# A table of shifted priorities in a kernel whose instruction order is made by a list scheduler

## The chip, the cores and the metric

The kernel runs on one core of a Trainium2 chip. The metric is the device time of one execution in microseconds; three runs of the kernel before gave 1033.35 as their median. Engines are named as in the profile: PE (TensorE), DVE (VectorE), ACT (ScalarE), POOL (GpSimd) and SP (SyncE, which here only issues DMAs).

## What is computed

Hash-masked attention for 4 batches of 8 heads (768 positions, 64 dimensions), and a gated two-layer product on its output. The weights come in as 64-bit floats.

```python
q_bits = (np.einsum('bhsd,dk->bhsk', q, proj) > 0)     # 6 bits, k likewise
mask = q_bucket[:, :, :, None] == k_bucket[:, :, None, :]
scores = np.where(mask, scale * q @ k.T, -1e9)
attn = exp(scores - max); attn /= attn.sum(-1) + 1e-9
x = (attn @ v).transpose(0, 2, 1, 3).reshape(B * S, H * D)   # 3072 x 512
out = (sigmoid(x @ w_gate) * (x @ w_val)) @ w_out            # inner width 1536
```

## The kernel before

**Two stages.** In the first, the heads are taken in 16 pairs, each pair in two groups of 384 query positions. A pair (`pair`) is loaded, q and k are transposed on PE (`turn`, L957), split into two parts of lower precision, and hashed (`hash_`, L980); DVE turns the hashes into bits (`bits_k` L998, `bits_q` L991). A group (`group`) has three blocks of queries times two heads: six scores tasks (L1043 and L1048, 8 matmuls each, into PSUM tile `sc`), for each a maximum on DVE (L1057, which also moves the scores into `e`) and an exponent on ACT (L1065); then the reciprocal of the sums (`inverse`, three small DVE instructions, L1072 to L1075), six tasks of 12 transposes (`turned`, L1098, tile `tp`), each copied by ACT or DVE (L1105, tile `ef`), and three values tasks of 8 matmuls (`values`, L1115, tile `pv`). The sum is copied (L1122, `xs`), scaled on POOL (L1125) and stored to `xd` in DRAM (L1128).

In the same stage the weights are turned from 64-bit floats into pairs of 32-bit ones (`floats`, `load_w`, `load_pair`; DVE, ACT and POOL), and the first two of the twelve 128-wide slices of the inner width are already multiplied for every (batch, group) whose attention is stored (`moe_early`, `product` L548 with tiles `zg` and `zv`, `out_product` L581 with tile `zo`). A product task is 3 matmuls, four of them a product; an output task is 3 matmuls, two for each of three row blocks.

The second stage (`products`) does the other ten slices for all batches by a Strassen-like scheme of seven products (L789, tiles `zA`, `zB`, `zD`) and output pieces (L581, tile `y`). Its weights stream in through POOL's DMA queue (L1213). Between the stages stands `switch`, which waits for the last attention store, closes the first stage's memory pools and opens the second's.

**What sets the order.** No instruction is issued where it is written. Every step is put into a `Plan` with `add`: a key, an engine (or a choice of two), a cost in ns, what it comes after, and which buffers it takes and gives. `order` then plays the whole program through in a model of the chip: whenever an engine is free, it takes the ready task with the lowest `(key, number)` whose buffers are free. PE's choice also counts a price for a change of kind (`LEAVE`, `BEGIN`) and stays in its tiling for a while (`PATIENCE`): scores and transposes use half the rows of the array, values half the columns, all else the whole array. The order in which tasks start in the model is the order in which the program is emitted; on the chip each engine then works through its queue in that order, waiting where data are not there.

Keys are formulas: about one unit for each of the 96 query blocks of the whole kernel (`t0 = i * NC + g * GT`), with offsets: scores `n`, maxima `n - 3`, exponents `n + 1.25`, transposes `t0 + LAG + 0.4 c`, the first values task of a group `t0 + LAG + 4`, and its other two `OPEN`, which is -1: a task that goes on with an open accumulation goes ahead of everything. Early products begin with 10000 and the number of their unit (8 units) and go on with `OPEN`; a second-stage chain has 20000 and its batch; the 60 warm-up matmuls at the start have 100000.

**Buffers.** Scores, transposes and hashes share three PSUM tiles of two banks (`two`). Values, early products and outputs share two single banks (`one`), of which an early product may have one (`moe`). A group's accumulation holds its bank from its first values task until the copy at L1122.

Of the kernel before, what the change touches and what calls it, by code (L numbers as in the profile page):

```python
# [40 lines left out]
RATE, LANDING = 240.0, 2000  # L41


class Task:


# [20 lines left out]
class Plan:  # L67
# [9 lines left out]

    def add(self, key, engine, ns=None, emit=None, after=(), take=(), give=(), tail=0, kind="all", behind=()):
        options = engine if isinstance(engine, list) else [(engine, ns, emit)]
        t = Task((key, len(self.tasks)), options, after, take, give, tail, kind, behind)  # L80
        self.tasks.append(t)
        return t

# [104 lines left out]
def lsh_attention_glu_kernel(ctx, tc, q, k, v, proj, w_gate, w_val, w_out, out):  # L188
# [107 lines left out]
    def busy():  # L296
# [6 lines left out]
        t=0, zt=0, ws0=0, ws1=0, ws2=0, xb=0, r0=0, r1=0, r2=0, x1=0, x4=0, x5=0, x6=0, wk2=0,  # L303
# [4 lines left out]
    add = plan.add  # L308
# [8 lines left out]
    def dma(key, nbytes, emit, engine="sp", slack=0, **kw):  # L317
        t = add(key, engine, 600, emit, tail=LANDING + int(nbytes / RATE), **kw)
        t.size, t.slack = nbytes, slack
        return t  # L320
# [7 lines left out]
    def floats(key, load, after, last, name):  # L328
# [38 lines left out]

        a = dma(key, 524288, load_, slack=3000 if last else 0, after=after, take=[place])
        b1 = add(key, "dve", 440, exponent, after=[a], take=["mid" + own])
        b2 = add(key, "act", 700, shifted, after=[b1])  # L370
        c1 = add(key, "dve", 440, mantissa, after=[b1])
        c2 = add(key, "dve", 700, whole, after=[c1])
# [214 lines left out]
    def moe_early(key, b, g, stored, pace):  # L587
# [50 lines left out]
        for j in range(J1):  # L638
            g_free[j] = prev

    def products(key, pair, prev, ends):


# [273 lines left out]
    def either(copied, n=1):  # L917
        return [
            ("act", 60 + 315 * n, lambda: copied(nc.scalar.copy)),
            ("dve", 70 + 400 * n, lambda: copied(nc.vector.tensor_copy)),  # L920
        ]

    def pair(i):
# [4 lines left out]
        two = slice(2 * hp, 2 * hp + 2)  # L928
# [36 lines left out]
        def high(n, copy):  # L965
            z[n + "h"], z[n + "l"] = (at.tile([P, S], F32R, name=f"{n}{x}{u}", tag=f"{n}{x}") for x in "hl")
            copy(ordered(z[n + "h"]), turned_(n))
# [16 lines left out]
        def hash_(n):  # L984
            z["hs", n] = ps2.tile([P, 2, 512], F32, name=f"h{n}{u}", tag="two")
            for j in range(2):
                hashed(z["hs", n], f"k{j}" if n == "k" else n, n, j)
# [7 lines left out]
        def bits_k(h):  # L995
            if h == 0:
                z["kb"] = at.tile([P, 2, GN], BF16, name=f"kb{u}", tag="kb")
            nc.vector.tensor_scalar(z["kb"][:, h], z["hs", "k"][:, h, :GN], thr_k[h], None, op0=ALU.is_gt)  # L998
# [5 lines left out]
        needs, last_turn = [], None  # L1004
        for m, n in enumerate("kq"):
            n_ = t0 - 6 + m
            last_turn = add(
                n_, "pe", NC * TH, lambda n=n: turn(n), after=[here[n], last_turn],
                take=["two"] + ["h"] * (m == 0), give=[n + "r"], kind="turn",
            )  # L1010
            a = add(n_, either(lambda copy, n=n: high(n, copy), 2), after=[last_turn])
# [3 lines left out]
        for m, n in enumerate("kq"):  # L1015
            n_ = t0 - 2.8 + m * 0.6
            a = add(n_, "pe", 6 * MM, lambda n=n: hash_(n), after=[needs[m]], take=["two"])
            if n == "k":
                needs += [
                    add(n_, "dve", 590, lambda h=h: bits_k(h), after=[a], give=["two"] * h) for h in range(2)  # L1020
                ]
            else:
                needs.append(add(n_, "dve", 990, bits_q, after=[a], give=["two"]))
        needs += swaps
# [2 lines left out]
        for g in range(NG):  # L1027
            group(i, g, z, needs, v_here)

    def group(i, g, z, needs, v_here):  # L1030
# [3 lines left out]
        gz = {}  # L1034

        def scores(t, h):

            c = slice((g * GT + t) * P, (g * GT + t + 1) * P)
            gz["sc", t, h] = sc = ps2.tile([P, 2, 512], F32, name=f"sc{u}_{t}_{h}", tag="two")
            for m, (a, x) in enumerate((("l", "h"), ("h", "l"), ("h", "h"))):  # L1040
                for j, rows in enumerate(halves):
                    q_ = z[("q" if j == h else "qs") + a]
                    nc.tensor.matmul(  # L1043
                        sc[:, j, :GN], q_[rows, c], z["k" + x][rows, h * GN : (h + 1) * GN],
                        start=(m == 0), stop=False, tile_position=(j * D, 0),
                    )
            for j, rows in enumerate(halves):
                nc.tensor.matmul(  # L1048
                    sc[:, j, :GN], z["qb"][rows, c], z["kb"][rows, h], start=False, stop=True, tile_position=(j * D, 0),
                )  # L1050

        def maximum(t, h):

            if h == 0:
                gz["st", t] = at.tile([P, 2], F32, name=f"st{u}_{t}", tag="st", bufs=stock["st"])
            gz["e", t, h] = e = at.tile([P, S], F32, name=f"e{u}_{t}_{h}", tag="e", bufs=stock["e"])
            nc.vector.tensor_scalar(  # L1057
                sp(e), gz["sc", t, h][:, :, :GN], -MASKED * SCALE, None, op0=ALU.min, op1=ALU.min,
                accum_out=gz["st", t][:, h : h + 1],
            )  # L1060

        def exponent(t, h):
            gz["su"] = sums[(i * NG + g) % len(sums)]
            e, st = gz["e", t, h], gz["st", t]
            nc.scalar.activation(  # L1065
                e, e, AF.Exp, bias=st[:, h : h + 1], scale=-1.0,
                accum_out=gz["su"][:, h * GT + t : h * GT + t + 1],
            )
# [61 lines left out]
        exps = []  # L1130
        for t in range(GT):
            n = t0 + t
            least = []
            for h in range(2):
                a = score_tasks[n] = add(
                    n + h * 0.5, "pe", 6 * MM // 2 + 165, lambda t=t, h=h: scores(t, h), after=needs + score_tasks.get("last", []),
                    take=["two", "e"] + ["st"] * (h == 0), kind="scores",
                    give=["h"] if g == NG - 1 and t == GT - 1 and h == 1 else [],
                )
                score_tasks["last"] = [a]  # L1140
                least.append(add(n - 3, "dve", 880, lambda t=t, h=h: maximum(t, h), after=[a], give=["two"]))
            for h in range(2):
                exps.append(add(
                    n + 1.25, "act", 1025, lambda t=t, h=h: exponent(t, h), after=[least[h]] + exps[:1],
                    take=["su"] if t == 0 and h == 0 else [], give=["st"] * (h == 1),
                ))
        n = t0 - 0.78
        a = add(n, "dve", 560, inverse, after=exps, take=["sv"], give=["su"])
        a = add(n, "sp", 600, told, after=[a], tail=2500, give=["sv"])
        spread_ = add(n, "sp", 1200, spread, after=[a], tail=3500, take=["rb"])  # L1150
        chunks, last = {}, None
        for c in range(NC):
            n = t0 + LAG + c * 0.4
            last = add(n, "pe", 2 * GT * TH, lambda c=c: turned(c), after=exps + [last], take=["two", "ef"],
                       give=["e"] * GT * 2 if c == NC - 1 else [], kind="turn")
            chunks[c] = add(n, either(lambda copy, c=c: whole(c, copy), 2), after=[last], give=["two"])
        n = t0 + LAG + 4
        prev = None
        for cs in [range(c, c + VB) for c in range(0, NC, VB)]:
# [3 lines left out]
                after=[prev, v_here] + [chunks[c] for c in cs], take=["one"] if first else [], kind="values",  # L1163
                give=["ef"] * VB + (["vr"] if final and g == NG - 1 else []),
            )
        a = add(n - 6, either(summed), after=[prev], take=["xs"], give=["one"])
        a = add(n - 4, "pool", 1230, divided, after=[a, spread_], give=["rb"])
# [7 lines left out]
    for i in range(len(heads)):  # L1175
        pair(i)
# [5 lines left out]
    for m, w in enumerate(order):  # L1182
        key = W_KEY + W_STEP * m + W_MORE * max(0, m - 3 * J1)
# [18 lines left out]
    def switch():  # L1202
# [5 lines left out]
                          give=["moe"] * 3 + [r for r, n in late_stock.items() for _ in range(n)])  # L1208
# [51 lines left out]
```

## Time and profile before

| | |
|---|---|
| median of three runs | 1033.35 us (1033.17 to 1033.66) |
| the profiled execution | 1032.77 us, of which the span of its instructions 1031.0 |
| granted TensorE clock | 0.999 |
| HBM | 177 GB/s over the span |
| largest groups | exponents L1065 178.7 us of ACT, maxima L1057 176.4 us of DVE, `y` L581 150.9 us of PE, `pv` L1115 140.6 us of PE |

A timeline row gives start, length, engine, line, operation, `out<-in`, and how many like it were merged; brackets hold the idle time before it and whose end ended that. Matmuls are pipelined, so lengths overlap, and the distance between two starts is what a task takes. A row of stretches gives, for a window, its length and then busy time and instructions of PE, PEld, DVE, ACT and POOL, the granted clock, the DMA share and GB/s. A row of groups gives `xcount`, then busy time and mean ns of one, then the idle time before them with its causes.

### The profile page before, as it was taken

The numbers are of one execution on the slowest core, as the hardware profiler recorded it, in microseconds if no ns is written. First come the engines' busy times: TensorE is split into PE (matmuls) and PEld (weight loads), VectorE is DVE, ScalarE is ACT, GpSimd is POOL, SyncE is SP. The second block draws the span as 40 slices with busy tenths as digits, with TensorE's granted clock in tenths as the row PEclk, the third lists the DMA queues.
The fourth block names the chain that finished last, engine by engine and source line by source line (L and its number), as shares of the span: only waits on it lengthen the run. The fifth ranks groups of instructions, "written<-read, shape, count | busy, mean of one in ns | idle before, by whom it ended". The sixth has DMA issues, their size and how long they took to land.

```text
span 1031.0 us, 20353 instructions
## 1 busy us (share of the span) xinstructions
PE 1008.5 (98%) x8172; PEld 803.3 (78%) x8172; DVE 665.1 (65%) x1257; ACT 563.4 (55%) x1024; POOL 235.9 (23%) x248
## 2 busy tenths in 40 slices
PE   9999999999999999999998999999999999999998
PEld 5666567676676676766677899999999999999997
DVE  6889898788888878777636646564326433553234
ACT  2777778787676766877745434443325232433231
POOL 2213456444544333552022000000000000000000
PEclk9999999999999999999999999999999999999999
DMA  8344466765766646544147977576445754366411
GB/s 214 88 127 132 139 186 195 249 181 172 237 198 193 195 166 201 188 159 162 38 143 308 385 285 285 207 255 222 183 167 194 253 216 164 143 242 244 168 72 62
DMA packets 114558, 196.36 MB, mean 190 GB/s; under 512 B 61216, under 2 KB 83744, under 8 KB 109344
## 3 DMA queue, kind: packets, MB, share of 16 engines
q1 hardware_dynamic: 108544, 121.66, 37.0%
q0 software_dynamic: 5760, 73.40, 19.3%
q8 instruction: 64, 1.05, 0.4%
q14 instruction: 30, 0.25, 0.1%
q10 hardware_dynamic: 160, 0.00, 0.0%
HBM read 140.51 MB, written 41.94 MB: 177 GB/s over the span
## 4 chain that ended last, share of the span: by engine, by line
PE 85%; DVE 8%; issue 3%; ACT 2%; DMA 1%; POOL 0%; SPq 0%; DVEq 0%; ACTq 0%; POOLq 0%
PE y L581 16%; PE pv L1115 11%; PE sc L1043 9%; PE zBg L789 8%; PE zBv L789 8%; PE tp L1098 5%; PE zDg L789 4%; PE zDv L789 4%; DVE e L1057 3%; PE zo L581 3%; PE zg L548 3%; PE sc L1048 3%; PE zv L548 2%; PE zAg L789 2%; PE zAv L789 2%
## 5 line engine op out<-in xcount | busy, mean ns | idle before, releaser
L1065 ACT ACTIVATE e<-e,st 128x768 f32<-128x768 f32 x192 | 178.7, 932 | 36.5 <-DVE e L1057 35.9
L1057 DVE TENSOR_SCALAR_CACHE_REDUCE e<-sc 128x768 f32<-128x768 f32 x192 | 176.4, 953 | 22.8 <-PE sc L1048 22.6
L581 PE MATMUL y<-wo,gh 128*128 128x512 f32 x480 | 150.9, 396 | 0.0
L1115 PE MATMUL pv<-ef,vr 128*64 128x384 f32 x768 | 140.6, 496 | 0.0
L1105 ACT COPY ef<-tp 128x768 f32<-128x768 f32 x117 | 92.1, 798 | 50.8 <-PE tp L1098 49.7
L1098 PEld LDWEIGHTS tp<-ident,e 64*128 64x128 f32 x2304 | 83.9, 139 | 31.5 <-issue 20.3
L581 PEld LDWEIGHTS y<-wo,gh 128*128 128x128 f32 x480 | 90.0, 187 | 15.4
L1098 PE MATMUL tp<-ident,e 64*128 64x64 f32 x2304 | 95.4, 226 | 2.4 <-DVE ef L1105 1.1
L789 PE MATMUL zBv<-x,wsv 128*128 128x384 f32 x480 | 96.5, 335 | 0.9 <-ACT t167v L797 0.9
L789 PE MATMUL zBg<-x,wsg 128*128 128x384 f32 x480 | 96.4, 335 | 0.6 <-ACT t167g L797 0.6
L581 PE MATMUL y<-wo,gl 128*128 128x512 f32 x240 | 93.2, 389 | 0.0
L1043 PE MATMUL sc<-kh,ql 64*128 64x384 f32 x192 | 85.9, 447 | 6.5 <-ACT ef L1105 2.4
L789 PEld LDWEIGHTS zBv<-x,wsv 128*128 128x128 f32 x480 | 85.4, 188 | 6.4 <-ACT t167v L797 1.3
L789 PEld LDWEIGHTS zBg<-x,wsg 128*128 128x128 f32 x480 | 85.4, 188 | 5.9 <-ACT t167g L797 0.9
L1115 PEld LDWEIGHTS pv<-ef,vr 128*64 128x64 f32 x768 | 48.4, 136 | 53.3 <-issue 47.5
L1105 DVE COPY ef<-tp 128x768 f32<-128x768 f32 x75 | 71.2, 953 | 27.2 <-PE tp L1098 26.5
L1043 PE MATMUL sc<-kh,qsl 64*128 64x384 f32 x192 | 85.9, 447 | 1.1 <-DVE ef L1105 1.0
L882 ACT CAST gh<-zt 128x384 fp32r<-128x384 f32 x80 | 40.7, 513 | 83.5 <-DVE zt L877 72.0
L1048 PE MATMUL sc<-kb,qb 64*128 64x384 bf16 x384 | 64.6, 333 | 0.0
L1043 PE MATMUL sc<-kl,qh 64*128 64x384 f32 x192 | 64.0, 333 | 0.0
L1043 PE MATMUL sc<-kl,qsh 64*128 64x384 f32 x192 | 64.0, 333 | 0.0
L1043 PE MATMUL sc<-kh,qsh 64*128 64x384 f32 x192 | 64.0, 333 | 0.0
(193 smaller groups left out, 2051.9 us busy)
## 6 DMA issues: line engine op xcount, KB each, us to landing
wsg<-kzg POOLq DMA_DIRECT2D x20, 1792.0 KB, 7.9
wsv<-kzv POOLq DMA_DIRECT2D x20, 1792.0 KB, 7.8
kzg<-wkg SPq DMA_DIRECT2D x10, 896.0 KB
kzv<-wkv SPq DMA_DIRECT2D x10, 896.0 KB
kr<-in_k_dram SPq DMA_DIRECT2D x64, 96.0 KB
qr<-in_q_dram SPq DMA_DIRECT2D x32, 192.0 KB
vr<-in_v_dram SPq DMA_DIRECT2D x16, 384.0 KB
qsh<-qh SPq DMA_DIRECT2D x32, 192.0 KB
```

Of the source, the lines that this page charges most:

```text
L548: nc.tensor.matmul(z["acc"][:, :GN], a[:, wc], x[xx][:, c, :], start=(c == 0 and i == 0), stop=(c == KC - 1 and i == 2),)
L581: nc.tensor.matmul(acc, a[:, slot, ts_], w, start=(first and i == 0), stop=(last and i == 2))
L789: nc.tensor.matmul(acc, streams[n, jp][:, c, wa, a_], X[x_][:, xa, c], start=first and c == 0 and i == 0, stop=c == 1 and i == 2, skip_gro ...
L882: nc.scalar.copy(side["h"][:, blk], w["z", blk])
L1043: nc.tensor.matmul(sc[:, j, :GN], q_[rows, c], z["k" + x][rows, h * GN : (h + 1) * GN], start=(m == 0), stop=False, tile_position=(j * D, 0),)
L1048: nc.tensor.matmul(sc[:, j, :GN], z["qb"][rows, c], z["kb"][rows, h], start=False, stop=True, tile_position=(j * D, 0),)
L1057: nc.vector.tensor_scalar(sp(e), gz["sc", t, h][:, :, :GN], -MASKED * SCALE, None, op0=ALU.min, op1=ALU.min, accum_out=gz["st", t][:, h : ...
L1065: nc.scalar.activation(e, e, AF.Exp, bias=st[:, h : h + 1], scale=-1.0, accum_out=gz["su"][:, h * GT + t : h * GT + t + 1],)
L1098: nc.tensor.transpose(tp[:, r, at_ : at_ + D], gz["e", t, h][rows, c * P : (c + 1) * P], ident[rows, rows], tile_position=(r * D, 0),)
L1105: copy(gz["ef", c].rearrange("p (n r d) -> p r n d", r=2, d=D), gz["tp", c][:, :, :GN].rearrange("p r (n d) -> p r n d", d=D),)
L1115: nc.tensor.matmul(gz["pv"][rows, :GN], z["v"][:, h, c], gz["ef", c][:, h * GN : (h + 1) * GN], start=(c == 0), stop=(c == NC - 1), tile_p ...
```

## The change

Every task's key is shifted by an entry of a table, in steps of 0.05, by the task's number (the count of `add` calls before it). The rest of the scheduler is as it was.

```diff
+UNIT = 0.05
+SHIFT = {
...
+    -42, 43: -1, 44: -1, 45: -1, 46: -1, 47: -1, 50: -1, 51: -1, 55: -1, 56: -122, 58: -1, 95: 244, 100: -7, 102:
+    -17, 103: -8, 106: -15, 108: -30, 137: -37, 139: -74, 141: -74, 143: -74, 145: -299, 147: -299, 149: -149,
...
+    207: 248, 211: -144, 219: -127, 223: -127, 225: -255, 232: -127, 236: -65, 238: -32, 240: -32, 242: -42,
...
+    21, 1502: 85, 1516: 42, 1549: 6, 1601: -15, 1609: 84, 1612: -30, 1904: -199163, 1910: -200473, 1920: 15,
+    1953: 625, 1969: 928, 1971: 928, 1979: 1416, 1980: 1, 2045: 705, 2048: -198326, 2062: -198574, 2063: 2024,
+    2083: -202609, 2113: 2184, 2204: 37, 2206: 2, 2237: 3, 2239: 24, 2241: 397737, 2250: 201066, 2258: -26,
+    2259: -19, 2260: -1, 2261: -1, 2266: 1, 2283: -3108, 2306: -1, 2328: -1, 2623: -1, 2907: 1, 3198: 1,
+}
...
-        t = Task((key, len(self.tasks)), options, after, take, give, tail, kind, behind)
+        m = len(self.tasks)
+        t = Task((key + SHIFT.get(m, 0) * UNIT, m), options, after, take, give, tail, kind, behind)
...
             if n == "k":
-                needs += [
-                    add(n_, "dve", 590, lambda h=h: bits_k(h), after=[a], give=["two"] * h) for h in range(2)
-                ]
+                for h in range(2):
+                    needs.append(add(
+                        n_, "dve", 590, lambda h=h: bits_k(h), after=[a] + needs[-1:] * h, give=["two"] * h
+                    ))
...
-            if h == 0:
+            if ("st", t) not in gz:
                 gz["st", t] = at.tile([P, 2], F32, name=f"st{u}_{t}", tag="st", bufs=stock["st"])
```

By the count of the `add` calls, the 255 entries fall on these tasks (a positive shift is a later key):

| tasks | earlier | later |
|---|---|---|
| warm-up matmuls (0 to 59) | 31 | 8 |
| transposes of `e` (L1098), of 192 | 56 | 8 |
| scores (L1043), of 192 | 17 | 15 |
| values (L1115), of 96 | 5 | 15 |
| q and k transposes (L957) and hashes (L980), of 64 | 20 | 7 |
| early products (L548) and outputs (L581), of 176 | 5 | 11 |
| other: DVE, ACT, POOL, SP, and one product of the second stage | 37 | 20 |

Of the five early parts that come earlier four are the first part of a product and one the first of an output: their key falls from 10000 and more to between -126 and 87, into the range of the attention tasks. Entry 95 is the `inverse` of the first group. Entry 2241 is the third part of the last unit's last product (key -1, now 19885.85); 2250 the first output part of its second row block (from 10007 to 20060.3); 2283 the first product of the second stage (from 20000 to 19844.6). Past task 2283 only five entries are left, each of one step.

The two other edits write down an order that equal keys gave before: the second of the two k-bits instructions comes after the first, and of the two maxima that share a tile, the first to be emitted makes it.

More of the change, by code (lines that the diff above doesn't have):

```diff
@@ L1143, in group @@
                 exps.append(add(
-                    n + 1.25, "act", 1025, lambda t=t, h=h: exponent(t, h), after=[least[h]] + exps[:1],
+                    n + 1.25, "act", 1025, lambda t=t, h=h: exponent(t, h), after=[least[h]] + exps[:1] + exps[-1:] * h,
                     take=["su"] if t == 0 and h == 0 else [], give=["st"] * (h == 1),
```

18 rows, old and new, of the table SHIFT are left out of this document.

## The prediction

> **What bounds the kernel now.** I read the page's head, then the stretches of the span, then TensorE's own timeline. The profiled execution took 1032.77 us, 0.58 under the median of 1033.35, with a span of 1031.0.
>
> ```profile
> span 1031.0 us, 20353 instructions
> PE 1008.5 (98%) x8172; PEld 803.3 (78%) x8172; DVE 665.1 (65%) x1257; ACT 563.4 (55%) x1024; POOL 235.9 (23%) x248
> PEclk9999999999999999999999999999999999999999
> PE 85%; DVE 8%; issue 3%; ACT 2%; DMA 1%; POOL 0%; SPq 0%; DVEq 0%; ACTq 0%; POOLq 0%
> ```
>
> PE is busy for 98% and carries 85% of the chain that ended last, at full clock throughout. The change neither adds nor removes a matmul, so it can only win what PE loses between matmuls. Where that is, the stretches say (columns: span, PE, PEld, DVE, ACT, POOL):
>
> ```profile
> 22.73:100.00 77.27, 74.73 (x912) 49.47 (x913) 67.84 (x136) 56.30 (x105) 16.04 (x12) 1.00 0.42 115
> 100.00:150.00 50.00, 47.09 (x559) 31.20 (x559) 44.78 (x88) 39.17 (x72) 22.06 (x18) 1.00 0.55 159
> 150.00:350.00 200.00, 197.34 (x2099) 135.92 (x2096) 170.23 (x324) 152.03 (x267) 97.38 (x98) 1.00 0.65 202
> 350.00:530.00 180.00, 177.33 (x1930) 121.91 (x1930) 133.28 (x260) 128.61 (x228) 61.12 (x60) 1.00 0.47 151
> 530.00:582.00 52.00, 46.26 (x235) 40.15 (x232) 27.64 (x38) 26.74 (x49) 12.54 (x13) 1.00 0.81 311
> 582.00:1000.00 418.00, 418.00 (x2189) 389.00 (x2189) 196.57 (x353) 149.99 (x288) 19.00 (x36) 1.00 0.59 214
> ```
>
> From 582 to 1000 PE idles for nothing: the second stage is a block of fixed length. Up to 582 PE idles 2.54 + 2.91 + 2.66 + 2.67 + 5.74 = 16.5 us. DVE is near its own limit early: 112.6 of 127.3 us up to 150 (88%).
>
> Busy time hides a second loss: the first matmul of a task waits for PE to change its tiling. Prices are distances between starts:
>
> ```profile
> 22.73 0.44 PE L1043 MATMUL sc<-kh,ql 64*128 64x384 f32 x1
> ...
> 23.41 0.47 PE L1043 MATMUL sc<-kh,qsl 64*128 64x384 f32 x1
> ...
> 24.11 0.47 PE L1043 MATMUL sc<-kh,ql 64*128 64x384 f32 x1
> ...
> 505.26 1.51 PE L1115 MATMUL pv<-ef,vr 128*64 128x384 f32 x8
> 506.70 0.44 PE L1043 MATMUL sc<-kh,ql 64*128 64x384 f32 x1
> ...
> 507.52 0.53 PE L1098 MATMUL tp<-ident,e 64*128 64x64 f32 x12
> 507.86 0.42 PE L1043 MATMUL sc<-kh,qsl 64*128 64x384 f32 x1
> ...
> 508.74 0.45 PE L548 MATMUL zg<-xh,we 128*128 128x384 f32 x1
> ...
> 511.05 0.97 PE L1098 MATMUL tp<-ident,e 64*128 64x64 f32 x24
> 511.95 2.80 PE L1115 MATMUL pv<-ef,vr 128*64 128x384 f32 x16
> 514.68 1.34 PE L1098 MATMUL tp<-ident,e 64*128 64x64 f32 x36
> ...
> 532.33 0.39 PE L581 MATMUL zo<-wo,gl 128*128 128x512 f32 x1
> ...
> 535.06 0.33 PE L548 MATMUL zg<-xh,we 128*128 128x384 f32 x1
> ...
> 539.25 0.33 PE L548 MATMUL zv<-xh,we 128*128 128x384 f32 x1
> ...
> 560.76 1.21 PE L789 MATMUL zBg<-x,wsg 128*128 128x384 f32 x6
> ```
>
> A scores task ahead of another takes 0.70 (23.41 to 24.11), ahead of a transpose 0.82 (506.70 to 507.52), ahead of a product 0.88 (507.86 to 508.74). A values task alone takes 1.44 (505.26 to 506.70), two in a row 1.36 each. A transpose task takes 0.45 in a run of two, but 0.34 ahead of scores; I take 0.40. A product part takes 0.52 (eight in 4.19), an output part 0.68 (four in 2.73). The last row is the first matmul of the second stage.
>
> ```profile
> L1043 PE MATMUL sc<-kh,ql 64*128 64x384 f32 x192 | 85.9, 447 | 6.5 <-ACT ef L1105 2.4 <-DVE ef L1105 1.7 <-DVE e L1057 1.4
> L1115 PE MATMUL pv<-ef,vr 128*64 128x384 f32 x768 | 140.6, 496 | 0.0
> L1098 PE MATMUL tp<-ident,e 64*128 64x64 f32 x2304 | 95.4, 226 | 2.4 <-DVE ef L1105 1.1 <-DVE e L1057 0.9
> L548 PE MATMUL zg<-xh,we 128*128 128x384 f32 x128 | 38.0, 351 | 0.6 <-ACT xh L519 0.6
> L581 PE MATMUL zo<-wo,gh 128*128 128x512 f32 x96 | 29.9, 393 | 0.0
> 22.73:560.76 538.03, 34.83 (x168) 28.57 (x168) 1.00 0.55 172
> 22.73:560.76 538.03, 15.26 (x336) 12.85 (x336) 1.00 0.55 172
> ```
>
> The last two rows are the stretch 22.73 to 560.76 for the hash and for the q/k transposes alone. With 192 scores, 96 values (8 matmuls), 192 transposes (12), 128 product parts (64 for zg, as many for zv) and 42 output parts (48 less the six behind 560.76), unbroken work is 192 x 0.70 + 96 x 1.36 + 192 x 0.40 + 128 x 0.52 + 42 x 0.68 + 34.8 + 15.3 = 487 us of 538. So **51 us are lost**: 16 idle (some of it behind 560.76), the rest in changes. I counted 357 changes of task kind in PE's timeline between the first and the last row above: about 0.1 each, as the single prices say.
>
> **The change part by part.** *39 of the 255 entries* reorder the 60 identical warm-up matmuls: nothing on the chip.
>
> *Held parts.* 15 values tasks and 11 parts of early products and outputs (five and six) get a later key; most had the key -1, "go on at once". Such a part can now lie beside its like, or fill a hole. What one saves is one excursion: 0.08 out of values (1.44 less 1.36) and up to 0.18 into it (0.88 less 0.70, the nearest row). 26 x 0.26 = 6.8 us if all hit; below nothing if each makes an excursion of its own. I take half, 3.4, since what surrounds them is mostly not shifted.
>
> *Transposes earlier.* 56 of 192 get an earlier key, so runs get longer. A removed change between them and another mode is worth about 0.09; 56 x 0.09 = 5.0. Half: 2.5. Between scores and transposes the pair of changes costs only (0.82 - 0.70) + (0.34 - 0.40) = 0.06. [...]
>
> *Earlier scores, turns, hashes; DVE, ACT and SP tasks.* These aim at the idle time. One can be seen at work: the sums' inverse of the first group (entry 95, key -0.78 to 11.42).
>
> ```profile
> 31.65 0.17 DVE L1072 TENSOR_SCALAR su<-su 128x6 f32<-128x6 f32 x1
> ...
> 32.21 0.92 DVE L1057 TENSOR_SCALAR_CACHE_REDUCE e<-sc 128x768 f32<-128x768 f32 x1
> ```
>
> It sits 0.56 us ahead of a maximum which frees a score bank, while DVE has no slack; later it is in nobody's way. Idle time up to 530 is 10.8 us. I take a third, 3.6, with ends of -3.6 (as much lost) and 10.8: DVE's own 88% stays. The 13 SP tasks pass only others of a queue that has 0% of the chain; should a q/k load or swap come late, its scores wait, some us at a time, inside the lower end.
>
> *The switch.* PE's idle time here, by its rows:
>
> ```profile
> 556.47 0.44 PE L548 MATMUL zv<-xh,we 128*128 128x384 f32 x1 [1.54 <-ACT ob L622]
> ...
> 562.88 0.50 PE L581 MATMUL zo<-wo,gl 128*128 128x512 f32 x1 [0.91 <-POOL gl L569]
> ...
> 572.06 1.31 PE L789 MATMUL zBg<-x,wsg 128*128 128x384 f32 x6 [0.57 <-ACT t167g L797]
> ...
> 580.59 1.31 PE L789 MATMUL zBv<-x,wsv 128*128 128x384 f32 x6 [0.95 <-ACT t167v L797]
> ```
>
> Entry 2250 sends four of the last unit's output parts (4 x 0.68 = 2.7) behind the second stage's own chain: they run in its holes, of which 0.57 + 0.95 = 1.5 are seen. Entry 2241 lets the first Strassen product go ahead of a product part; that holds back a stream tile, the POOL queue that waits to refill it and the gl behind it, against which stands the 0.91. Ends -1 and 1.5; I take 1.2.
>
> *The explicit orders.* Both name what the one queue does already. In the plan the second k-bits instruction can now be parted from the first, holding a score bank longer: 16 times 0 to 0.1; I take 0.3 in all.
>
> Sum: 3.4 + 2.5 + 3.6 + 1.2 - 0.3 = 10.4. On the profile's own time 1032.77 - 10.4 = 1022.4; at the median **1022.9**. All terms at their best: 24, or 1009.
>
> **The rivals.** *Larger, 1013:* the half and third that I took are nearer four fifths; what speaks for it is that a lost 51 us is much to search in; against it, that DVE's 88% is no matter of order.
>
> *Port contention, 1029.5.* DVE and GpSimd slow each other down:
>
> ```profile
> L885 DVE TENSOR_TENSOR gl<-zt,gh 128x384 fp32r<-128x384 f32 x80 | 43.7, 553 | 15.6 <-ACT gh L882 15.6
> L522 DVE TENSOR_TENSOR xl<-xr,xh 128x384 fp32r<-128x384 f32 x14 | 11.5, 838 | 4.4 <-ACT xh L519 4.4
> ```
>
> The same operation and shape takes 553 in the second stage, where POOL works little, and 838 in the first. The plan has one price for either. If the new order brings some 23 more DVE operations beside POOL and PE waits for each, 23 x 0.285 = 6.6 is given back. [...]
>
> *No change, 1032.5:* the table does not do what it says in chip time: shifts of a twentieth break ties, and what is won early returns as waits at the switch, whose chain of loads and casts is the same. Against it: the switch follows the last attention store, so it moves along.
>
> *Slower, 1037.5, by held banks.* Values, products and outputs share two PSUM banks. A held part keeps its bank; whoever needs one then waits for a copy, as at 556.47 for 1.54. At about 1.0 each (below that row, since scores and transposes can fill some of it), the 26 held parts break even at ten exposed waits; at fifteen it is 15 - 10.4 = 4.6 slower. Against it: this is one of few such waits now.
>
> **How the numbers follow.** About 0.2% (2.1 us) is what a measurement can tell from no change. Chances: forecast (1016 to 1028) 0.54, larger 0.14, contention (up to 1031.3) 0.12, no change 0.09, slower 0.11. So faster 0.80, same 0.09, slower 0.11. The range 1011.5 to 1033.0 leaves out the far end of the large gains and the slower case.
>
> **What would show it.** The first zBg starts near 550 instead of 560.76 and what follows keeps its 470 us; changes of kind fall from 357 to some 320; idle time up to the switch falls by 3 to 4. The forecast is wrong if zBg starts within 2 us of 560.76, if waits on ACT's or DVE's bank copies (ob, xs, sig) show up ahead of zv, zg, zo or pv, or if DVE's xl and exponent pieces get longer.

## The result, and the profile after

The kernel after took 1027.08 us as the median of four runs (1026.65 to 1027.85), beside 1033.51 for the kernel before: a ratio of 0.9937 with a 95% interval of 0.992 to 0.9954. That is 6.4 us faster, three times the 0.2% that can be told from no change. The forecast was 10.4 us.

One thing has to be added to the change as it was told above. There is a third hunk in the diff, and it is one of the two explicit orders: the second of a block's two exponents now comes after the first.

```diff
-    after=[least[h]] + exps[:1],
+    after=[least[h]] + exps[:1] + exps[-1:] * h,
```

So the two explicit orders are the k-bits and the exponents; the edit of the `st` tile only follows from letting either maximum come first.

The profiled execution of after took 1027.25 us. The head of its page and the chain that ended last:

```profile
span 1025.2 us, 20353 instructions
PE 1005.3 (98%) x8169; PEld 802.7 (78%) x8172; DVE 674.7 (66%) x1265; ACT 563.1 (55%) x1023; POOL 235.7 (23%) x241
PE 84%; DVE 8%; ACT 3%; DMA 3%; issue 1%; SPq 1%; POOL 0%; ACTq 0%; DVEq 0%; POOLq 0%
```

PE has the same matmuls (the trace holds three records fewer) and 3.2 us less busy time (1008.5 before). DVE has eight instructions more (1257 before: the steps that may run on either of two engines fell out a little differently), and 9.6 us more (665.1 before). How much of this the eight steps need is the first thing to find out. Now the stretches of the span, in the columns of those of before:

```profile
22.73:100.00 77.27, 75.48 (x923) 49.76 (x921) 67.27 (x134) 59.02 (x108) 18.97 (x13) 1.00 0.48 128
100.00:150.00 50.00, 49.09 (x562) 33.21 (x562) 45.82 (x92) 41.49 (x75) 23.91 (x19) 1.00 0.54 157
150.00:350.00 200.00, 197.72 (x2145) 137.59 (x2145) 172.91 (x323) 152.56 (x271) 97.24 (x97) 1.00 0.65 203
350.00:530.00 180.00, 176.60 (x1899) 120.76 (x1896) 143.92 (x269) 126.83 (x224) 60.04 (x58) 1.00 0.47 150
530.00:582.00 52.00, 46.89 (x244) 42.23 (x243) 30.04 (x47) 25.96 (x47) 10.60 (x11) 1.00 0.87 339
582.00:1000.00 418.00, 418.00 (x2191) 389.22 (x2190) 190.60 (x342) 149.44 (x286) 18.47 (x35) 1.00 0.57 209
```

PE's idle time up to 582 is the length of each window less its first number: 13.5 us, where it was 16.5. Up to 150 it fell from 5.45 to 2.70; from 150 to 530 it rose from 5.33 to 5.68; at the switch it fell from 5.74 to 5.11. Last, the two rows of PE's timeline by which every kernel below is placed, the last values task and the first matmul of the second stage:

```profile
524.23 1.51 PE L1146 MATMUL pv<-ef,vr 128*64 128x384 f32 x8
...
555.04 1.20 PE L819 MATMUL zBg<-x,wsg 128*128 128x384 f32 x6
```

The second stage starts 5.72 us earlier than at 560.76, and what follows it takes 1025.2 - 555.04 = 470.2, as before (1031.0 - 560.76 = 470.2). The whole change happened in the first stage. In before the last values task was this row, so that at the end of the attention the new order was ahead by 4.95:

```profile
529.18 1.51 PE L1115 MATMUL pv<-ef,vr 128*64 128x384 f32 x8
```

Counted in PE's timeline between 22.73 and the first zBg, changes of task kind fell from 357 to 311 (the plan's four kinds: scores, all transposes, values, all else). But those between scores and transposes, which keep the tiling, fell from 120 to 64; all others, which are the changes of tiling, rose from 237 to 247.

### The profile page after: what moved, and what is told of

It is laid out like the page before. It is cut to its first block, busy times and chain, and to the rows that moved or that the text cites. A ratio compares the mean times of both kernels' runs of the same rounds, so it can differ in the third digit from the quotient of the medians.

```text
span 1025.2 us, 20353 instructions
## 1 busy us (share of the span) xinstructions
PE 1005.3 (98%) x8169; PEld 802.7 (78%) x8172; DVE 674.7 (66%) x1265; ACT 563.1 (55%) x1023; POOL 235.7 (23%) x241
## 4 chain that ended last, share of the span: by engine, by line
PE 84%; DVE 8%; ACT 3%; DMA 3%; issue 1%; SPq 1%; POOL 0%; ACTq 0%; DVEq 0%; POOLq 0%
PE y L611 16%; PE pv L1146 10%; PE sc L1074 9%; PE zBv L819 8%; PE zBg L819 8%; PE tp L1129 6%; PE zDv L819 4%; PE zDg L819 4%; PE sc L1079 3%; PE zo L611 3%; PE zv L578 2%; PE zg L578 2%; PE zAv L819 2%; DVE e L1088 2%; PE zAg L819 2%; DMA B<-xd 1%
## 5 line engine op out<-in xcount | busy, mean ns | idle before, releaser
L1088 DVE TENSOR_SCALAR_CACHE_REDUCE e<-sc 128x768 f32<-128x768 f32 x192 | 174.3, 951 | 18.8 <-PE sc L1079 18.0
```

The lines of the kernel that those rows point to most:

```text
L1088: nc.vector.tensor_scalar(sp(e), gz["sc", t, h][:, :, :GN], -MASKED * SCALE, None, op0=ALU.min, op1=ALU.min, accum_out=gz["st", t][:, h : ...
```

## The experiments

Each run stands beside runs of the kernel before on its own chip; ratios are to that kernel, with 95% intervals. Two theories stood at the start. The first: the order as such is better than 6.4 us, and DVE working beside POOL takes a part back, which is where DVE's 9.6 us come from. Its rival: contention is the same tax on any order, and the forecast's terms were simply too large. Beside them stood the question what the table and the explicit orders do each alone.

### Contention: POOL's reading steps made into fills

In each kernel every step of POOL that reads SBUF writes a constant of the same shape instead; both runs leave these parts of the computation out.

```diff
+            if eng is nc.gpsimd:
+                return eng.memset(f(z["mf"]), 0.25)
...
-            nc.gpsimd.tensor_scalar(z["q"], z["q"], -SCALE, None, op0=ALU.mult)
+            nc.gpsimd.memset(z["q"], 0.0125)
```

On the order of before:

> The order of before, but every elementwise instruction of POOL that reads SBUF is a fill of the same tile that reads nothing (this leaves out the low parts, the scaling of q and the division, so the output is not the reference's). Both theories: faster, 1026 to 1031, since DVE's stretched instructions (about 17 us more than their usual length in all) get their usual length. It is the base for the next run.

On the order of after:

> The same fills in the changed order. Theory 'port contention eats the gain' (DVE is stretched by about 26 us in the changed order against 17 in the old, which the plan does not price): without it the two orders lie 10 to 13 us apart, so about 1016. Rival 'the plan's prices of PE are off' (a change of tiling costs on the chip what the plan does not charge, the new order has as many of them): the distance stays 5 to 7 us, so about 1022.

Measured: 1033.62 on the order of before (0.9999, 0.9989 to 1.0008), which is nothing where both theories had expected at least 2 us, and 1022.25 on that of after (0.9895, 0.9878 to 0.9912), 4.8 less than after. The time of the second is the one that the rival named, but its base had not moved; what separates the two theories is the distance between the two orders. The pages of the two, before's order first:

```profile
PE 1007.7 (98%) x8170; PEld 805.3 (78%) x8172; DVE 650.8 (63%) x1257; ACT 562.5 (55%) x1024; POOL 101.1 (10%) x248
```

```profile
PE 1002.7 (98%) x8169; PEld 804.6 (79%) x8172; DVE 651.8 (64%) x1265; ACT 562.6 (55%) x1023; POOL 100.8 (10%) x241
```

Without POOL's reads DVE needs 651 to 652 in either order, so the eight instructions net 1.0. And POOL's steps cost DVE 665.1 - 650.8 = 14.3 in the old order and 674.7 - 651.8 = 22.9 in the new: of the 9.6 us, 8.6 are this. Where they sit is seen in two groups; `su` in before first, then both in after, then both with the fills:

```profile
L1072 DVE TENSOR_SCALAR su<-su 128x6 f32<-128x6 f32 x32 | 9.6, 301 | 6.1 <-ACT e L1065 6.1
```

```profile
L552 DVE TENSOR_TENSOR xl<-xr,xh 128x384 fp32r<-128x384 f32 x15 | 14.3, 976 | 6.0 <-ACT xh L549 6.0
L1103 DVE TENSOR_SCALAR su<-su 128x6 f32<-128x6 f32 x32 | 12.4, 386 | 2.4 <-ACT e L1096 2.4
```

```profile
L564 DVE TENSOR_TENSOR xl<-xr,xh 128x384 fp32r<-128x384 f32 x15 | 8.1, 555 | 15.4 <-ACT xh L559 15.3
L1115 DVE TENSOR_SCALAR su<-su 128x6 f32<-128x6 f32 x32 | 5.4, 168 | 1.9 <-ACT e L1108 1.8
```

The sums' `su` step works on six numbers per partition and takes 168 ns in after's order with fills. In after one of them takes 1.79 us, and POOL's step, which runs over the same moment, shows why it did (DVE's timeline, then POOL's):

```profile
421.24 1.79 DVE L1103 TENSOR_SCALAR su<-su 128x6 f32<-128x6 f32 x1
...
423.42 0.92 DVE L1088 TENSOR_SCALAR_CACHE_REDUCE e<-sc 128x768 f32<-128x768 f32 x1
```

```profile
420.90 2.10 POOL L514 TENSOR_TENSOR wkg<-mfg,wkg 128x896 fp32r<-128x896 f32 x1 [2.48 <-ACT wkg L511]
```

POOL's step ends at 423.00, `su` at 423.03: it waited to the end of POOL's step and not for a share of it. So did every one of these `su` steps that took over 0.3 us, six in before and seven in after: each ends 0.02 to 0.04 us after the end of a POOL step. A maximum stands behind this one in DVE's queue. What the two engines share no run here shows; "port" is the author's word for it, in the texts and in the model.

What PE loses by it is read at the end of the attention. The last values task starts at 525.99 in before's order with fills and at 518.60 in after's:

```profile
525.99 1.51 PE L1127 MATMUL pv<-ef,vr 128*64 128x384 f32 x8
...
547.32 0.69 PE L560 MATMUL zg<-xh,we 128*128 128x384 f32 x1 [7.17 <-ACT xh L529]
...
562.20 1.21 PE L801 MATMUL zBg<-x,wsg 128*128 128x384 f32 x6
```

```profile
518.60 1.51 PE L1158 MATMUL pv<-ef,vr 128*64 128x384 f32 x8
...
539.50 0.69 PE L590 MATMUL zg<-xh,we 128*128 128x384 f32 x1 [6.74 <-ACT xh L559]
...
541.91 0.52 PE L590 MATMUL zg<-xl,we 128*128 128x384 f32 x1
542.23 0.52 PE L590 MATMUL zg<-xh,we 128*128 128x384 f32 x1
...
553.57 1.20 PE L831 MATMUL zBg<-x,wsg 128*128 128x384 f32 x6
```

The fills win 3.2 us for the old order and 5.6 for the new. The new order is ahead by 7.4 there instead of 4.95: contention takes some 2.4 us of its gain. By the medians it is more, 11.4 between the two orders instead of 6.4, or 5.0 (by the ratios 0.0104 instead of 0.0063, or 4.2); the profiled run with after's order took 1024.28, 2.0 above its median, so its rows may understate it. The rival, the same tax on any order, falls. With one reserve: the fills also shorten POOL's own steps (236 to 101 us), so what is shown is the cost of POOL's steps, not of their reads alone.

The old order won its 3.2 us and then had none of it at 562.20. The bracket says where it went, a hole of 7.17 at the switch; it is taken up in the last section.

### The table and the explicit orders, each alone

The orders alone:

```diff
-SHIFT = {
...
+SHIFT = {}
```

> The explicit orders alone, with an empty table. Theory 'nothing but names': the queues hold what equal keys gave before, so 1033.5, within 1. Theory 'any edge reshuffles the plan': the two edges make the second instruction of each pair ready some 0.13 later in the plan, a neighbour slips in between, and all that follows is ordered anew; then the time moves by several us, more likely up, to some 1037, and a part of the table's work is to repair it.

Measured: 1040.25, 1.0068 (1.0049 to 1.0086), some 7 us slower than before. In the profiled run, the slowest of the four, the second stage starts at 570.24. A part of the loss comes early, as the stretches show:

```profile
22.73:100.00 77.27, 73.37 (x879) 48.28 (x876) 64.04 (x128) 53.57 (x99) 16.37 (x12) 1.00 0.43 117
100.00:150.00 50.00, 45.85 (x547) 30.29 (x546) 44.90 (x91) 38.07 (x70) 18.01 (x15) 1.00 0.52 153
```

PE idles 8.05 us up to 150, beside 5.45 in before; from 150 to 530 it is 7.30 beside 5.33. Two orders that a reader would take for what the queue does anyway thus cost some 7 us when the keys stay as they were. What each of the two costs was not tried.

The table alone:

```diff
-    after=[a] + needs[-1:] * h, give=["two"] * h
+    after=[a], give=["two"] * h
...
-    after=[least[h]] + exps[:1] + exps[-1:] * h,
+    after=[least[h]] + exps[:1],
```

> The whole table without the two explicit orders. 'A sum of parts': the orders alone cost some 6 us, so the table without them would win 6 more, 1021. 'A fitted whole': the table was fitted to a plan with them, so without them little of the gain is left, 1031 to 1036.

Measured: 1037.52, 1.0029 (1.0019 to 1.0038): slower than before too. Either half alone loses, together they win 6.4. If the parts added up, the two together would be some 10 us slower.

The model in which the order is made says the same. Played through by the kernels' own `order`, it starts the second stage at 560.6 us in before, at 565.5 with the orders alone, at 562.2 with the table alone and at 546.6 with both; the chip did so at 560.76, 570.24, 564.74 and 555.04. So the orders cost time in the plan already, the halves do not add there either, and of the 14 us that the plan promises up to here for the whole change the chip gave 5.7. (From there to its end the plan gives the two kernels with the table 5.5 us less; on the chip that part is the same for all four.)

Parts of the table. First without its 64 entries for the transposes of `e` (56 earlier, 8 later), then without the 39 for the warm-up matmuls, which are all the same instruction; the shorter table is written here as a filter:

```diff
+SHIFT = {k: v for k, v in SHIFT.items() if k not in TRANSPOSES}
```

> The changed kernel without the 64 entries of the transposes of e. Theory 'a sum of parts' (the prediction's): it loses that part's term, 2.5 or less, and stays well under the kernel before, about 1029. Theory 'a fitted whole' (each key orders all that follows, so the table is worth something only complete): all of the gain is gone, 1033 or more, as likely as not near 1037.

```diff
+SHIFT = {k: v for k, v in SHIFT.items() if k >= 60}
```

> The changed kernel without the 39 entries of the warm-up matmuls, which are all alike on the chip though the plan gives the first eight a higher price. Theory 'they fit the plan alone': same as the changed kernel, 1027 within 1. Theory 'a fitted whole': the first ready times shift in the plan and some of the gain goes, 1029 or more.

Without the transposes' entries: 1061.17, 1.0267 (1.0246 to 1.0287), 27 us slower than before. Its stretches from 100 on:

```profile
100.00:150.00 50.00, 45.78 (x517) 29.14 (x515) 44.48 (x84) 34.96 (x65) 20.80 (x16) 0.97 0.59 164
150.00:350.00 200.00, 192.68 (x2010) 133.32 (x2012) 168.96 (x316) 144.93 (x258) 91.33 (x89) 0.98 0.62 191
350.00:530.00 180.00, 172.76 (x1840) 116.79 (x1838) 145.43 (x273) 123.34 (x219) 65.31 (x63) 0.98 0.51 158
```

PE idles for 4.22 + 7.32 + 7.24 = 18.8 us here, against 6.6 in after, and the granted clock is below 1.00 in each (0.97, 0.98, 0.98). So the remaining entries without these are far worse than no table at all. Without the warm-up entries: 1029.8, 0.9959 (0.9944 to 0.9973). The interval overlaps that of after by 0.001, so the times alone make a loss likely but do not show it. That these 39 entries change more than the warm-up is seen in PE's rows, after first, then without the entries:

```profile
11.71 0.54 PE L987 MATMUL tq<-ident,qr 64*128 64x64 f32 x12
...
13.52 0.52 PE L1010 MATMUL hk<-kh,hwk0l 128*128 128x384 f32 x1
...
22.40 0.44 PE L1074 MATMUL sc<-kh,ql 64*128 64x384 f32 x1
```

```profile
11.88 0.53 PE L985 MATMUL hk<-kh,hwk0l 128*128 128x384 f32 x1
...
13.21 0.59 PE L962 MATMUL tq<-ident,qr 64*128 64x64 f32 x12
...
24.29 0.44 PE L1049 MATMUL sc<-kh,ql 64*128 64x384 f32 x1
```

The matmuls are one and the same instruction, but the plan prices the first eight double, and on the chip too the first ones take longer: in before the first eight start 0.40 to 0.43 apart and the next eight 0.21 to 0.23. Where the plan's dear ones stand decides what is ready when in it. Without the entries the first hash goes ahead of the second transposes and the first scores start 1.89 us later; the plan has the second stage 2.0 us later (548.7).

These four runs point the same way. The table's entries have no price one by one that could be added up.

### The epsilon added to the sums

The small `su` step above is the addition of 1e-9 to the sums. Leaving it out takes 32 DVE instructions away.

```diff
-            nc.vector.tensor_scalar_add(some, some, EPS)
```

On the order of after, then on that of before:

> The changed order without the DVE instruction that adds 1e-9 to the sums of the exponents (left out; the sums are at least 1). It took 12.4 us of DVE in 32 instructions, up to 2.0 each, beside POOL. Theory 'port contention': these are among the worst collisions, so 2 to 4 us faster than the changed kernel, about 1024. Rival: the reciprocal behind it is in nobody's way, within 1 of 1027.

> The kernel before without the DVE instruction that adds 1e-9 to the sums (left out). In the changed order that was worth about 2.4 us. If the collision with POOL is what made it dear, it is worth less here, where those instructions took 9.6 us in all and not 12.4: 0 to 1.5 us, 1032 to 1033.5. If it is DVE's time as such: 2 to 3 us, about 1031.

Measured: 1024.2 (0.9914, 0.9897 to 0.993) on after, 0.0023 below after's ratio, and 1031.6 (0.998, 0.9971 to 0.999) on before. So in the medians it is worth 2.4 us in the new order and 2.1 in the old; the first interval overlaps that of after (from 0.992). Were its collisions with POOL all that counts, the new order should gain twice as much: its step takes 386 ns where the fills leave 168, 218 too long, and in the old order 301 where they leave 190, 111 too long. Measured is 1.1 times, with intervals too wide to decide between the two. What is shown is that the step costs some 2 us in the old order; that it does so in the new is likely. That its collisions carry the new order's whole loss is not shown.

### Two further tables, from a plan that prices the port

In these kernels the scheduler's model makes certain DVE and POOL steps that read SBUF (kind `port`) wait for each other, each for at most 1.3 us (`HOLD`). Four prices of POOL steps are changed too. Under this model two tables were searched for, table b from no shifts at all.

```diff
+                    if t.kind == "port" and e in port:
+                        wait = max(0, port["dve" if e == "pool" else "pool"] - now)
+                        port[e] = now + wait + min(ns, HOLD)
+                        ns += wait
```

> The scheduler is given a price for the shared port (a DVE and a POOL instruction that both read SBUF go one after the other) and POOL's measured times, and a new table is fitted to that plan by the same kind of search, over the first stage. Theory 'the gain was lost to port contention that the plan does not price': more of the fitted gain arrives, 1020 to 1025. Rival 'any fitted table keeps a third': in the plan it moves the first product of the second stage by 15 us, a third is 5, so 1028 to 1029 or worse. DVE's instructions should be stretched by less than the 25.5 us of the changed kernel if the plan has the port right.

> The same plan with another table, searched from no shifts at all. It has the same length in the plan within 0.5 us, so what differs between this and the run before is what a plan cannot tell: within 2 us of it if the plan is right, more if not.

Measured: table a 1036.49, 1.0039 (1.0021 to 1.0057), slower than before; table b 1024.45, 0.991 (0.9895 to 0.9924). The scheduler's own model put the two within 0.2 us of each other at the start of the second stage (554.0 and 554.2); the chip puts them 12 apart. The stretches of table a, then of table b:

```profile
150.00:350.00 200.00, 194.80 (x2086) 135.29 (x2084) 169.02 (x317) 149.92 (x265) 96.75 (x95) 1.00 0.63 196
```

```profile
150.00:350.00 200.00, 199.05 (x2164) 137.89 (x2161) 172.75 (x328) 156.97 (x273) 100.12 (x98) 1.00 0.66 204
```

From 150 to 350 PE idles 5.2 us with table a and 0.95 with table b (2.28 in after). DVE's busy time is 671.1 us for 1254 instructions with a and 665.8 for 1257 with b, beside 674.7 for 1265 in after: it is below after's in both, so by this sign it is not more collisions that make a slow. The longest waits of PE, table a first:

```profile
PE tp L1285 <- DVE e L1244: 4.0, 8, 1.3
PE sc L1230 <- DVE qb L1177: 3.7, 2, 3.4
```

```profile
PE sc L1221 <- DVE e L1235: 2.2, 5, 1.2
```

That pricing the port gives the gain back is therefore not shown: table b agrees with it, table a speaks against it, and the changed prices of POOL steps were not tried apart. What in the orders makes a and b differ was seen only as these waits, and stays open.

The same two tables without the addition of 1e-9:

> The first of the two tables without the DVE instruction that adds 1e-9 to the sums (left out). In the old and in the changed order that was worth 2.1 and 2.4 us; the same here, 2 to 2.5 us under the first of these runs.

> The second of the two tables, which was the fastest so far (ratio 0.991), without the DVE instruction that adds 1e-9 to the sums (left out). Three orders gave 2.0 to 4 us for that, so 1020 to 1022 and under every kernel here. If DVE is no longer on the path in this order (PE idles for 11.5 us in it, against 16.5 before), 1023.5 to 1024.5.

Table a gave 1032.46 (0.9991, 0.9981 to 1.0002), table b 1022.05 (0.9891, 0.9871 to 0.9911). In the medians that is 4.0 and 2.4 us for the addition. So leaving it out pays in the medians of every order tried; clear of the intervals it is in two, before's and table a's. Of the kernels that do the whole computation, table b (0.991) has the fastest median here; its interval overlaps that of after by 0.0004.

## Why the prediction was right, and where its sum was off

- **What bounds it** was right. In every kernel above the rest after the first zBg took 469 to 471 us; all that happened, happened ahead of it.
- **The sign, the range and the idle time** came as put: idle time down by 3.0 (3 to 4 were given). But it was not where the prediction looked for all of it. Up to 530 it fell by 2.4 where 3.6 was taken, all of it ahead of 150; the switch was to give 1.2 and gave 0.6.
- **The warm-up entries, "nothing on the chip".** This was wrong as a mechanism: they change the order of the first tasks and move the first scores by 1.89 us. What they are worth in the end is 2 us in the plan and not settled by the times.
- **Held parts, 3.4: the term that was not there.** It was to come out of fewer changes into and out of values and products. Those changes did not fall; all but the scores/transposes pairs rose from 237 to 247. In microseconds no run measured it. Taking half of 26 savings assumed that a held part lies beside its like, and the working had no row for that.
- **Transposes earlier, 2.5.** The 56 changes that went are 28 pairs between scores and transposes. At the 0.06 per pair of the prediction that is 1.7 us, below the 2.5 that it took. No run measured it by itself. What a change of tiling costs is seen in before at the products: the first matmul of a part takes 0.44 us behind scores or transposes and 0.33 to 0.34 behind work of its own tiling. A scores task's first takes 0.42 behind transposes and 0.47 behind other scores, in the median. Only changes within one tiling became fewer. By the price above these are worth little.
- **The explicit orders, 0.3: the step that failed worst.** "Both name what the one queue does already" is true of the old order in the queue, not of the plan that makes the queue. Alone they cost some 7 us on the chip and 4.9 in the plan. The sum's form failed with it: it added the parts, while the runs show that they do not add.
- **Port contention, 6.6 as a rival with 0.12.** By the fills POOL's steps cost DVE 22.9 us in the new order and 14.3 in the old, and the signs that the prediction named came: the `xl` pieces got longer (838 to 976 ns), and two of the three exponent pieces did (`exg` most, 684 to 838 ns). It goes both ways: in before POOL's `gl` at 171.58, which starts while DVE's `xl` runs from 171.53 to 172.07, takes 1.36 us, and the shortest 0.99. By the prediction's own words the longer pieces made the forecast wrong, though the time lies in its range. Its size is 2.4 us by the last values task, 5.0 by the medians, against 23 x 0.285 = 6.6. It was written as a case of its own; it belonged into the sum as a term. With 2.4 to 5.0 given back, 10.4 becomes 5.4 to 8.0, around the 6.4 measured. That is luck in part: the rest of the sum holds a gain from held parts that did not come and puts at 0.3 what alone costs some 7.
- **Slower by held banks** was not seen: ahead of zv, zg, zo and pv PE has one wait of note on a bank's copy, the first row here (1.8), as before had one of 1.54:

```profile
PE zg L578 <- ACT sig L630: 1.8, 1, 1.8
PE sc L1074 <- DVE ef L1136: 1.3, 3, 0.7
PE sc L1074 <- DVE e L1088: 1.0, 2, 0.6
```

Of the 5.72 us, idle time is 3.0 and the pairs are about 1.7 by their price. The last 1.0 is not assigned.

## What to carry to other kernels

When a list scheduler makes the order, look up what an edit of priorities or dependences does to the whole order, not to the tasks it names: here two halves that each lose made a gain, and two dependences that look harmless cost some 7 us alone. The plan itself can be played through for each half ahead of any run; up to the second stage it had the sign of all three cases right, though not their size. Tell changes between kinds of work by what they cost before counting them: 28 pairs that went come to under 2 us by their single prices. And where a new order brought more POOL work beside DVE, DVE's busy time showed it: of its 9.6 us more, eight more instructions net 1.0 and POOL's steps 8.6. Put that difference into the sum as a term, and let the chip, not the plan, choose between orders that the plan puts within a microsecond: the two tables, 0.2 us apart in it, came out 12 apart.

## What the hardware showed that was not expected

A gain in the attention can be lost at the switch. In both kernels with fills PE stood still there for some 7 us. The waits of ACT in after's order with fills, and then three windows of 10 us of it:

```profile
ACT xh L559 <- DMA xr<-xd: 8.9, 1, 8.9
```

```profile
530.00:540.00 10.00, 3.26 (x18) 2.94 (x18) 0.61 (x2) 1.06 (x3) 1.48 (x4) 0.89 1.02 407
540.00:550.00 10.00, 10.00 (x44) 9.31 (x44) 5.28 (x7) 5.53 (x11) 0.00 (x0) 0.77 0.26 96
550.00:560.00 10.00, 9.96 (x52) 8.88 (x51) 7.84 (x10) 7.25 (x13) 1.37 (x3) 1.00 0.65 227
```

The first window shows what PE waits for: the 16 DMA engines are full (share 1.02, 407 GB/s), the load of `xr` that the last products need lands late, and ACT waits 8.9 us for it. PE comes back at 539.50, but the granted clock of the first two windows is 0.89 and 0.77: from 541.91 to 542.23 a product's matmul takes 0.32, where 0.18 is usual, as these rows of the same timeline show:

```profile
526.53 0.33 PE L590 MATMUL zg<-xl,we 128*128 128x384 f32 x1
526.71 0.51 PE L590 MATMUL zg<-xh,we 128*128 128x384 f32 x2
```

From 545.75 to 545.92 it takes 0.17 again. In before's order with fills it is the same: from 549.73 to 550.05 such a matmul takes 0.32, behind the hole of 7.17, and the granted clock is 0.76 from 540 to 550 and 0.90 from 550 to 560. Ahead of the hole it is 1.00 in both (520 to 530 here, 530 to 540 there). So the hole costs more than its length: PE is busy for the whole of the second window, and a mean clock of 0.77 makes that, as an estimate, 2.3 us of lost work. That the hole is what lowers the clock was read from these rows and not tried by itself.

The load may be late because of the stream's fetches, and the fills bring these forward: with its own steps done sooner, POOL issues the first two fetches 0.31 us ahead of the load of `xr` in before's order (531.20 and 531.51) and 0.33 ahead in after's (523.80 and 524.13). In the kernel before the load went first (535.00 and 535.30), and in after the fetch was 0.08 ahead; neither had such a wait. This was read from the rows and not tried by itself.
